# First attention: GpSimd scales the probabilities of 22 units, and scores and turned squares rotate through four and three banks

## The chip, the cores and the metric

The kernel runs on one core of a Trainium2 chip. The metric is device time in microseconds (us), the median of a few executions; lower is better. The engines are named as the profile names them: PE is TensorE (matmuls; PEld its weight loads), DVE is VectorE, ACT is ScalarE, POOL is GpSimd, SP is the engine whose queue starts most of the transfers. PSUM is the memory that PE writes and that DVE and ACT read; the kernel divides it into eight banks.

## The reference

Attention over 4 batches, 8 heads, 768 positions and a head size of 64, in which a position sees itself, the 127 positions before it (the window) and the first 4 positions (the sinks). The result is laid side by side by head (3072 rows of 512) and goes through a gated projection with matrices that arrive as 64-bit floats.

```python
scores = scale * np.matmul(q, k.transpose(0, 1, 3, 2))
keep = is_sink | in_window
scores = np.where(keep, scores, -1000000000.0)
a = np.exp(scores - np.max(scores, axis=-1, keepdims=True))
a = a / (np.sum(a, axis=-1, keepdims=True) + 1e-09)
x = (a @ v).transpose(0, 2, 1, 3).reshape(B * S, H * D)
out = ((x @ w_a) * (x @ w_b)) @ w_out
```

## The kernel before

**Chunks.** The rows are worked in eight chunks of one batch each; the first is batch 0, blocks 0 to 3 of 128 rows (`CHUNKS`). `run` computes the attention of the first chunk by itself (`alone=True`), and from then on the projection of chunk c (`moe`) with the attention of chunk c+1 spread between its matmuls. So the first attention is the only one that has no projection beside it; only the preparation of the first weights and the first products of the projection reach into its end.

**A unit** of the first attention is one head and one block of 128 rows: 8 heads by 4 blocks, 32 units, numbered n = 0 to 31 in the order head by head. Block 0 sees 128 columns (a narrow unit, n divisible by four: 8 of 32); the others see 264 columns: the block before, 8 sink columns and the block itself (24 wide units). `scores` (L601 and on) does for one unit:

- L610, PE: the scores, into a PSUM bank. The banks "s" and "a" take turns, so the scores of unit n+2 wait until those of unit n have been read.
- L617, DVE: adds the mask, takes the extreme of each row, and writes the masked scores `p` to SBUF (one operation and a short one that reads its accumulator).
- L619, ACT: the exponential in place, with the sum of each row beside it.
- L621 and L622, DVE: the sum plus 1e-9, and its reciprocal (one column each).
- L624, DVE: `p` times that reciprocal, in place: the scaling.
- L631, POOL, in blocks 2 and 3 alone (16 of the 32 units): copies the 8 scaled sink columns to `sc`.

`transposes` (L634 and on) turns the scaled `p` on PE (L645; one square for a narrow unit, two for a wide one) into a bank, "t" and "b" in turn, and ACT copies the bank to `pt` (L646). After each second head `av` multiplies the turned squares with the values (L426, 16 matmuls) and ACT copies the product to `xf` (L657); `sinks_t` turns the sink columns (L666, bank "t") and `sinks_av` adds their part (L677 on PE, L679 on DVE). `split_x` then makes two parts of each `xf` for the projection (L720 on ACT, L721 on DVE).

**Order.** `pipeline` issues scores(n), then what is due of `av` and the sinks, then transposes(n-3). That is the order of the code; the framework's scheduler then sets, before the run, the order in which each engine takes its instructions (in the trace L617 of a unit stands ahead of L622 of an earlier one, and L721, which stands behind the whole attention in the code, runs at 21.68 us). At run time each engine takes its own in that order and waits where an input or a buffer isn't ready. Functions marked `keep_in_program_order` keep their order among themselves.

**Banks.** The eight banks are "s", "a", "t", "b", "av", "o0", "o1" and "o2". The projection uses "a" and "b" for its two first products and "o0", "o1", "o2" and "av" for its results; the attention of later chunks uses "s" and "t". During the first attention "o0" to "o2" have held only the warming matmuls at the very start.

**Weights.** From step k = 24 (`STEP0`) of the first attention on, every third step also prepares weights: `weight_bits` (L327 and L329 on DVE, L328 on ACT), `weight_sum` (L336, DVE), `weight_high` (L341, ACT), `weight_low` (L346, DVE). Step k is the one that issues the scores of unit k.

Of the kernel before, what the change touches and what calls it, by code (L numbers as in the profile page):

```python
# [7 lines left out]
F32 = mybir.dt.float32  # L8
# [5 lines left out]
ALU = mybir.AluOpType  # L14
# [5 lines left out]
P = 128  # L20
# [7 lines left out]
SW = 2 * P + NS  # L28
# [5 lines left out]
STEP0, STEPS = 24, 3  # L34
# [182 lines left out]
class Fast:  # L217
# [348 lines left out]
    def parts_exact(self, b, t0, nt, xf, alone, heads, bank):  # L566

        nc = self.nc
        tag = f"{b}_{t0}"
        s0 = max(t0 - 1, 0)  # L570
        nb = t0 + nt - s0
        kw = nb * KB - NS
        late = [i for i in range(nt) if t0 + i >= 2]
        units = [(h, i) for h in heads for i in range(nt)]
        preps, state, sc, vss, skt = {}, {}, {}, {}, {}

        def do_prep(h):
            if h not in heads:
                return
            u = f"{tag}_{h}"  # L580
            if alone:
                pool, at = (self.ld, dict(tag="io", bufs=NIO)) if h % 2 else (self.sp, dict(tag="ks"))
                k = pool.tile([P, MK], F32, name=f"kx{u}", **at)
                q = self.mo.tile([P, nt * P], F32, tag=f"x{'hl'[h % 2]}{h // 2}", name=f"qx{u}", bufs=1)
            else:
                k = self.sp.tile([P, MK], F32, tag="ks", name=f"kx{u}")
                q = self.sp.tile([P, 3 * P], F32, tag=("qh", "ql")[h % 2], name=f"qx{u}")
            nc.sync.dma_start(k[:, :kw], self.kD[b, h, :, s0 * KB:s0 * KB + kw])
            nc.sync.dma_start(q[:, :nt * P], self.qT[b, h, :, t0 * P:(t0 + nt) * P])
            if h % 2 == 0:  # L590
                v = self.sp.tile([P, 2, MB, D], F32, tag="vv", name=f"vx{u}")
                nc.sync.dma_start(v[:, :, :nb], self.vB[b, h // 2, :, :, s0:s0 + nb])
                if late:
                    vs = self.sp.tile([2 * NS, P], F32, tag="vs", name=f"vsx{u}")
                    c = h // 2 % 2
                    nc.sync.dma_start(vs, self.vS[b, h // 4, c * 2 * NS:(c + 1) * 2 * NS, c])
                    vss[h // 2] = vs
            else:
                v = preps[h - 1][2]
            preps[h] = k, q, v  # L600

        def scores(h, i):
            k, q, _ = preps[h]
            t = t0 + i
            u = f"{tag}_{h}_{i}"
            c0 = (max(t - 1, 0) - s0) * KB
            w = SW if t else P
            n = units.index((h, i))
            ps = self.ps.tile([P, SW], F32, tag="sa"[n % 2] if alone else "s", name=f"s{u}")
            nc.tensor.matmul(ps[:, :w], lhsT=q[:, i * P:(i + 1) * P], rhs=k[:, c0:c0 + w], start=True, stop=True)  # L610
            if alone and n % 5 > 2:
                p = self.mo.tile([P, SW], F32, tag=("gh", "gl")[n % 5 - 3], name=f"p{u}")
            else:
                p = self.at.tile([P, SW], F32, tag="p", name=f"p{u}")
            st = self.at.tile([P, 4], F32, tag="st", name=f"st{u}")
            m = (self.m0, self.m1)[t] if t < 2 else self.mg
            nc.vector.tensor_tensor_reduce(out=p[:, :w], in0=ps[:, :w], in1=m, scale=-0.0625, scalar=BIG,  # L617
                                           op0=ALU.add, op1=ALU.min, accum_out=st[:, 0:1])
            nc.scalar.activation(p[:, :w], p[:, :w], AF.Exp, bias=st[:, 0:1], scale=-1.0,  # L619
                                 accum_out=st[:, 1:2])  # L620
            nc.vector.tensor_scalar(st[:, 2:3], st[:, 1:2], 1e-9, None, op0=ALU.add)  # L621
            nc.vector.reciprocal(st[:, 3:4], st[:, 2:3])  # L622
            if alone:
                nc.vector.tensor_scalar(p[:, :w], p[:, :w], st[:, 3:4], None, op0=ALU.mult)  # L624
            else:
                nc.scalar.mul(p[:, :w], p[:, :w], st[:, 3:4])
            state[h, i] = p
            if i in late:
                if h % 2 == 0:
                    sc[h // 2, i] = self.at.tile([P, 2, NS], F32, tag=f"sc{i % 3}", name=f"sc{u}", bufs=2)  # L630
                (nc.gpsimd.tensor_copy if alone else nc.scalar.copy)(sc[h // 2, i][:, h % 2, :], p[:, P:P + NS])  # L631

        def transposes(h, i):
            p = state.pop((h, i))  # L634
            t = t0 + i
            u = f"{tag}_{h}_{i}"
            n = units.index((h, i))
            if alone:
                tp = self.ps.tile([P, 2, P], F32, tag="tb"[n % 2], name=f"t{u}")
            else:  # L640
                tp = self.half_bank(bank, 0, f"t{u}")
            k = max(2 * i - (t0 == 0), 0)
            parts = [p[:, :P]] if t == 0 else [p[:, :P], p[:, P + NS:]]
            for m, part in enumerate(parts):
                nc.tensor.transpose(tp[:, m, :], part, self.ident)  # L645
            nc.scalar.copy(self.turned()[:, h % 2, k:k + len(parts), :], tp[:, :len(parts), :])  # L646

        def av(h):
            if h % 2 == 0:
                return  # L650
            v = preps[h][2]
            if alone:
                ps = self.ps.tile([P, 4, P], F32, tag="av", name=f"av{tag}_{h}")
            else:
                ps = self.half_bank(bank, 1, f"av{tag}_{h}")
            self.values(ps, v, t0, nt)
            nc.scalar.copy(xf[h // 2][:, :nt * P].rearrange("p (c q) -> p c q", q=P), ps[:, :nt, :])  # L657

        def sinks_t(pr):
            n = len(late)  # L660
            if alone:
                tp = self.ps.tile([P, 4, P], F32, tag="t", name=f"skt{tag}_{pr}")
            else:
                tp = self.half_bank(bank, 0, f"skt{tag}_{pr}")
            for k, i in enumerate(late):
                nc.tensor.transpose(tp[:2 * NS, k, :], sc[pr, i].rearrange("p a b -> p (a b)"), self.ident)  # L666
            s = self.at.tile([2 * NS, 3 * P], F32, tag="sct", name=f"sct{tag}_{pr}", bufs=1)
            nc.vector.tensor_copy(s[:, :n * P].rearrange("p (c q) -> p c q", q=P), tp[:2 * NS, :n, :])
            skt[pr] = s

        def sinks_av(pr, _):
            n = len(late)
            if alone:
                ps = self.ps.tile([P, 4, P], F32, tag="av", name=f"sk{tag}_{pr}")
            else:
                ps = self.half_bank(bank, 1, f"sk{tag}_{pr}")
            nc.tensor.matmul(ps[:, :n, :], lhsT=vss[pr], rhs=skt.pop(pr)[:, :n * P], start=True, stop=True)  # L677
            xs = xf[pr][:, late[0] * P:nt * P].rearrange("p (c q) -> p c q", q=P)
            nc.vector.tensor_tensor(xs, ps[:, :n, :], xs, op=ALU.add)  # L679

        return do_prep, scores, transposes, av, sinks_t, sinks_av

    def pipeline(self, units, nt, late, do_prep, scores, transposes, av, sinks_t, sinks_av, lag, group, early):
# [264 lines left out]
```

## Time and profile before

| | us |
|---|---|
| median of 3 executions (771.41 to 772.18) | 771.99 |
| the profiled execution | 771.08 |
| its span in the trace | 769.4 |
| PE busy in the span | 756.9 (98%) |
| DVE, ACT, POOL busy | 396.2, 420.7, 240.8 |

The span is what the trace covers of the profiled execution; 1.7 us of its time lie around it. The page has parts: busy time by engine; the span in slices, with the TensorE clock that was granted; the DMA queues; the chain of work that ended last, followed back from the last instruction; groups of instructions by line with the mean duration of one and the idle time ahead of them. The trace can also be asked for stages (busy time of each engine in a stretch), for waits (who waited for whom) and for the instructions in order of time. A duration there runs from start to end of one instruction; neighbours overlap at their ends, so what one costs its engine is often better read from the distance of two starts. Ends of matmuls are modelled, so a busy PE may still have room.

### The profile page before, as it was taken

The page shows a single profiled execution, that of the slowest core. Times are in us where ns is not written, and L with a number is a line of the kernel's source. Part 1 is how long each engine was busy: PE and PEld are TensorE (multiplying, and loading weights), DVE is VectorE, ACT ScalarE, POOL GpSimd, SP SyncE. Part 2 cuts the span into 40 slices and gives each one's busy share as a digit, 9 for nine tenths or more (in the row PEclk, how much of TensorE's full clock was granted, in tenths as well). Part 3 has the DMA queues.
Part 4 walks back from the last instruction along what each step waited for, and adds up shares of the span by engine and source line. Part 5 has one row for each costly group of instructions (what it writes and reads, how often), then busy time and mean ns, then how long its engine had stood idle before and what let it go on. Part 6 is the DMA issues. An engine that isn't in the chain of part 4 may idle for free.

```text
span 769.4 us, 13051 instructions
## 1 busy us (share of the span) xinstructions
PE 756.9 (98%) x4341; PEld 661.8 (86%) x4341; DVE 396.2 (52%) x1407; ACT 420.7 (55%) x1257; POOL 240.8 (31%) x304
## 2 busy tenths in 40 slices
PE   8999999999999999999999999999999999999997
PEld 4668777789889998999999999999998999899996
DVE  7888999955543443354433454234443445333221
ACT  5875668656645665365434554356663545444431
POOL 1100000244514544165531645224533444102110
PEclk9989999999999999999999999999999999999999
DMA  9996301141221342311211211213333212015511
GB/s 326 340 351 223 128 12 56 55 132 50 60 72 47 120 138 82 125 36 47 59 59 52 60 42 32 63 55 104 111 108 108 67 52 69 1 42 191 167 54 43
DMA packets 44567, 75.78 MB, mean 98 GB/s; under 512 B 4592, under 2 KB 24016, under 8 KB 44496
## 3 DMA queue, kind: packets, MB, share of 16 engines
q1 hardware_dynamic: 41440, 69.40, 27.7%
q10 hardware_dynamic: 3024, 5.51, 1.9%
q8 instruction: 35, 0.57, 0.3%
q14 instruction: 36, 0.29, 0.1%
q0 software_dynamic: 32, 0.00, 0.0%
HBM read 68.60 MB, written 6.29 MB: 97 GB/s over the span
## 4 chain that ended last, share of the span: by engine, by line
PE 96%; DVE 2%; issue 1%; ACT 0%; DMA 0%; POOLq 0%; DVEq 0%; ACTq 0%
PE a L739 26%; PE o L748 26%; PE b L739 26%; PE av L426 5%; PE s L487 5%; PE s L610 2%; PE t L527 1%; PE t L533 1%; PE t L645 1%; DVE p L617 1%; PE t L426 1%; PE skt L548 1%; PE sk L560 0%; DMA nw_raw<-in_nw_dram 0%; DVE p L624 0%
## 5 line engine op out<-in xcount | busy, mean ns | idle before, releaser
L739 PE MATMUL a<-xh,w 128*128 128x384 f32 (+2 forms) x768 | 215.9, 344 | 0.0
L739 PE MATMUL b<-xh,w 128*128 128x384 f32 (+2 forms) x768 | 214.2, 342 | 0.0
L748 PE MATMUL o<-w,gh 128*128 128x512 f32 x576 | 185.3, 403 | 0.0
L739 PEld LDWEIGHTS a<-xh,w 128*128 128x128 f32 x768 | 139.2, 189 | 5.9 <-issue 0.5
L739 PEld LDWEIGHTS b<-xh,w 128*128 128x128 f32 x768 | 139.2, 189 | 3.9 <-issue 0.2
L739 PE MATMUL a<-xl,w 128*128 128x384 f32 (+2 forms) x384 | 129.8, 338 | 0.0
L739 PE MATMUL b<-xl,w 128*128 128x384 f32 (+2 forms) x384 | 129.2, 336 | 0.0
L769 POOL TENSOR_TENSOR gl<-g,gh 128x384 fp32r<-128x384 f32 x60 | 61.0, 1017 | 217.0 <-ACT gh L767 213.3
L764 DVE TENSOR_TENSOR g<-b,g 128x384 f32<-128x384 f32 (+2 forms) x96 | 53.5, 557 | 146.3 <-PE b L739 123.2
L748 PEld LDWEIGHTS o<-w,gh 128*128 128x128 f32 x576 | 103.4, 188 | 19.0 <-issue 0.3
L748 PE MATMUL o<-w,gl 128*128 128x512 f32 x288 | 113.7, 395 | 0.0
L767 ACT CAST gh<-g 128x384 fp32r<-128x384 f32 (+2 forms) x96 | 49.2, 512 | 85.4 <-DVE g L764 83.8
L497 ACT ACTIVATE p<-p,st 128x264 f32<-128x264 f32 (+1 forms) x152 | 65.4, 430 | 50.3 <-DVE st L495 49.6
L758 ACT COPY g<-a 128x384 f32<-128x384 f32 (+2 forms) x96 | 45.3, 472 | 74.7 <-PE a L739 70.1
L739 PEld LDWEIGHTS a<-xl,w 128*128 128x128 f32 x384 | 72.5, 189 | 2.9 <-issue 0.4
L739 PEld LDWEIGHTS b<-xl,w 128*128 128x128 f32 x384 | 72.4, 189 | 2.1 <-issue 0.3
L748 PEld LDWEIGHTS o<-w,gl 128*128 128x128 f32 x288 | 54.1, 188 | 13.6 <-DVE gl L769 0.9
L375 POOL TENSOR_SCALAR ks<-kr 64x400 fp32r<-64x400 f32 (+1 forms) x48 | 28.2, 587 | 106.6 <-DMA kr<-in_kT_dram 103.4
L375 POOL TENSOR_SCALAR qh<-qr 128x384 fp32r<-128x384 f32 x48 | 25.3, 527 | 108.3 <-PE s L487 72.9
L378 POOL TENSOR_TENSOR ks<-kr,ks 64x400 fp32r<-64x400 f32 (+1 forms) x48 | 57.8, 1204 | 3.8
L499 DVE TENSOR_SCALAR st<-st 128x1 f32<-128x1 f32 x152 | 23.2, 153 | 69.0 <-ACT p L497 68.7
L505 ACT ACTIVATE p<-p,st 128x128 f32<-128x128 f32 x96 | 38.7, 403 | 35.1 <-DVE st L500 34.8
(141 smaller groups left out, 1124.2 us busy)
## 6 DMA issues: line engine op xcount, KB each, us to landing
qr<-in_qT_dram SPq DMA_DIRECT2D x48, 192.0 KB, 2.4
raw<-in_wa_dram SPq DMA_DIRECT2D x12, 512.0 KB, 5.9
raw<-in_wb_dram SPq DMA_DIRECT2D x12, 512.0 KB, 6.9
raw<-in_wo_dram SPq DMA_DIRECT2D x12, 512.0 KB, 7.2
chk_a<-in_wa_dram SPq DMA_DIRECT2D x24, 256.0 KB, 3.1
chk_b<-in_wb_dram SPq DMA_DIRECT2D x24, 256.0 KB, 3.1
chk_o<-in_wo_dram SPq DMA_DIRECT2D x24, 256.0 KB, 3.0
out_dram<-os ACTq DMA_DIRECT2D x21, 256.0 KB, 2.2
```

What stands on the lines that cost most here:

```text
L375: self.nc.gpsimd.tensor_scalar(o, i, 1.0, 1.0, op0=ALU.mult, op1=ALU.mult)
L378: (self.nc.vector if self.no_gpsimd else self.nc.gpsimd).tensor_tensor(o, i, high.bitcast(F32), op=ALU.subtract)
L426: self.tc.keep_in_program_order(self.nc.tensor.matmul(ps[e * D:(e + 1) * D, i0:i1, :], lhsT=v[:, e, blk, :], rhs=pt[:, e, sl:sl + i1 - i0, :],
L487: nc.tensor.matmul(ps[:, :w], lhsT=q[:, i * P:(i + 1) * P], rhs=ks[:, c0:c0 + w], start=m == 0, stop=m == 1)
L497: nc.scalar.activation(p[:, :w], p[:, :w], AF.Exp, bias=st[:, 0:1], scale=-1.0, accum_out=st[:, 1:2])
L505: nc.scalar.mul(p[:, NS:KB], p[:, NS:KB], st[:, 3:4])
L739: nc.tensor.matmul(ps[:, :n], lhsT=w[:, ksl], rhs=x[:, :n], start=kk == 0 and i == 0, stop=kk == NK - 1 and i == 2)
L748: nc.tensor.matmul(outs[i], lhsT=g[:, sl], rhs=w, start=j == 0 and k == 0, stop=j == NJ - 1 and k == 2)
L758: nc.scalar.copy(g[:, :n], pa[:, :n])
L764: nc.vector.tensor_tensor(g[:, :n], pb[:, :n], g[:, :n], op=ALU.mult)
L767: nc.scalar.copy(gh[:, :n], g[:, :n])
L769: e.tensor_tensor(gl[:, :n], g[:, :n], gh[:, :n].bitcast(F32), op=ALU.subtract)
```

## The change

The scores of the first attention rotate through four banks ("a", "o0", "o1", "s") where they took turns in two ("s", "a"), and the turned squares through three ("o2", "t", "b") where they took turns in two ("t", "b"). The scaling (L624) of the units n = 0 to 21 is done by POOL; that of the units 22 to 31 stays on DVE. Only the first attention has `alone` set; nothing else changes.

```diff
-            ps = self.ps.tile([P, SW], F32, tag="sa"[n % 2] if alone else "s", name=f"s{u}")
+            ps = self.ps.tile([P, SW], F32, tag=("a", "o0", "o1", "s")[n % 4] if alone else "s", name=f"s{u}")
...
             if alone:
-                nc.vector.tensor_scalar(p[:, :w], p[:, :w], st[:, 3:4], None, op0=ALU.mult)
+                e = nc.gpsimd if n < STEP0 - 2 else nc.vector
+                e.tensor_scalar(p[:, :w], p[:, :w], st[:, 3:4], None, op0=ALU.mult)
             else:
...
             if alone:
-                tp = self.ps.tile([P, 2, P], F32, tag="tb"[n % 2], name=f"t{u}")
+                tp = self.ps.tile([P, 2, P], F32, tag=("o2", "t", "b")[n % 3], name=f"t{u}")
```

## Rows read from the trace of the kernel before

**Rows 1.** the page: the whole span, and each engine's busy time in it

```profile
span 769.4 us, 13051 instructions
...
PE 756.9 (98%) x4341; PEld 661.8 (86%) x4341; DVE 396.2 (52%) x1407; ACT 420.7 (55%) x1257; POOL 240.8 (31%) x304
```

**Rows 2.** stages: PE, PEld, DVE, ACT, POOL busy (instructions); clock, DMA share, GB/s

```profile
7.00:18.00 11.00, 10.33 (x57) 6.41 (x58) 10.40 (x66) 9.05 (x35) 1.15 (x6) 1.00 1.05 394
...
32.00:40.00 8.00, 6.14 (x39) 3.44 (x37) 7.57 (x36) 7.10 (x25) 1.38 (x3) 0.96 1.00 384
...
120.00:128.00 8.00, 8.00 (x47) 6.15 (x45) 7.80 (x16) 6.45 (x15) 0.00 (x0) 1.00 0.01 2
```

**Rows 3.** TensorE's waits from 6 to 150 us: total, times, longest

```profile
PEld s L610 <- DVE st L617: 4.0, 9, 1.5
...
PE s L610 <- DVE st L617: 1.6, 3, 1.1
```

**Rows 4.** the chain that ended last: start us, us, what

```profile
14.43 0.22 PE t L645 x2
...
15.64 0.38 PE skt L666 x2
...
16.02 1.73 PE av L426 x16
...
18.23 0.45 PE s L610 x2
...
18.68 0.62 PE sk L677 x2
...
25.44 1.66 PE av L426 x16
...
33.76 1.66 PE av L426 x16
...
46.64 1.66 PE av L426 x16
```

**Rows 5.** VectorE in order of time: start us, us, engine line operation

```profile
23.07 0.42 DVE L617 CUSTOM_DVE_ANT_0 p<-s,mg 128x264 f32<-128x264 f32 x1
...
23.42 0.35 DVE L624 TENSOR_SCALAR p<-p,st 128x264 f32<-128x264 f32 x1
...
23.69 0.15 DVE L622 RECIPROCAL st<-st 128x1 f32<-128x1 f32 x1
```

**Rows 6.** groups from 6 to 42.5 us: count, busy us, mean ns, idle before

```profile
L624 DVE TENSOR_SCALAR p<-p,st 128x264 f32<-128x264 f32 x22 | 7.6, 350 | 0.1
...
L619 ACT ACTIVATE p<-p,st 128x264 f32<-128x264 f32 x24 | 12.4, 516 | 1.6 <-DVE st L617 1.5
...
L646 ACT COPY pt<-t 128x256 f32<-128x256 f32 x22 | 8.0, 369 | 3.0 <-PE t L645 2.9
```

**Rows 7.** GpSimd's groups over the whole span, same columns

```profile
L375 POOL TENSOR_SCALAR qh<-qr 128x384 fp32r<-128x384 f32 x48 | 25.3, 527 | 108.3 <-PE s L487 72.9 <-issue 33.9 <-DMA qr<-in_qT_dram 0.6
...
L375 POOL TENSOR_SCALAR vs<-vsr 128x256 fp32r<-128x256 f32 x12 | 5.3, 445 | 31.1 <-DMA vsr<-in_vS_dram 16.4 <-issue 8.4 <-PE sk L560 6.3
...
L378 POOL TENSOR_TENSOR ql<-qr,qh 128x384 fp32r<-128x384 f32 x48 | 49.1, 1023 | 2.2
...
L631 POOL COPY sc<-p 128x8 f32<-128x8 f32 x16 | 4.3, 267 | 37.1 <-DVE p L624 16.7 <-DVE st L621 16.5 <-DVE st L622 3.9
```

**Rows 8.** one GpSimd copy, and VectorE's work at that moment (order of time)

```profile
34.91 0.86 POOL L631 COPY sc<-p 128x8 f32<-128x8 f32 x1 [2.58 <-DVE p L624]
...
34.71 0.67 DVE L336 CUSTOM_DVE_ANT_0 wf<-raw,wf 128x1024 uint16<-128x1024 uint16 x1
```

**Rows 9.** the end of the first attention: VectorE, TensorE, and a stage

```profile
40.37 0.35 DVE L624 TENSOR_SCALAR p<-p,st 128x264 f32<-128x264 f32 x1
...
40.86 0.66 PE L645 MATMUL t<-ident,p 128*128 128x128 f32 x2 [1.85 <-DVE p L624]
...
40.00:46.00 6.00, 5.09 (x15) 3.21 (x16) 5.87 (x14) 4.05 (x11) 0.78 (x2) 0.50 1.02 385
```

## Prediction

> **What bounds the kernel now.** I began with the page. PE is busy for 756.9 of 769.4 us [rows 1], so the change can win only where PE is not at its rate, and the first 50 us are the only place where that lasts. The stages show it: in the first attention PE, DVE and ACT all look nearly full (7 to 18 us), near its end DVE is at 7.57 of 8 us and PE at 6.14, and in the first projection PE has 8.00 of 8 with DVE close behind it [rows 2]. A busy PE has modelled ends, though, so I worked out its real need from the chain, where each piece stands at the distance of its successor: two matmuls for the scores of a wide unit 0.45 us, two squares 0.22, and for each second head 1.66 for the values, 0.62 and 0.38 for the sinks [rows 4]. Eight units (two heads, six wide, two narrow at about half) need 6 x 0.45 + 2 x 0.23 + 6 x 0.22 + 2 x 0.11 + 1.66 + 0.62 + 0.38 = 7.4 us. The value products start at 16.02, 25.44, 33.76 and 46.64 us [rows 4]: eight units took 9.4, 8.3 and 12.9 us. So PE was at its rate for only 79% and 89% of the two early stretches.
>
> What else could bound those two? DVE: from start to start a wide unit costs 0.35 for L617, 0.27 for the scaling with the accumulator read [rows 5], and about 0.14 for the two one-column operations (estimated from the 23.69 row's 0.15 with its overlap); a narrow one about 0.5. Eight units are 6 x 0.76 + 2 x 0.5 = 5.6, with some 1.4 for the sinks and L721: 7.0. ACT: 0.516 and 0.369 for a wide unit by their means [rows 6], which count overlaps twice, some 0.6 for a narrow one, 1.1 for the copy of the product and the first part: at most 7.6. All three lie below 9.4 and 8.3. So no engine's total bounds the early stretch; it is the handing over. PE waits 4.0 and 1.6 us (weight loads and matmuls) for L617 to release a score bank [rows 3]: with two banks PE can't put more than two units in front of DVE, and during the 2.7 us of values and sinks DVE and ACT run dry, after which PE waits for them in turn.
>
> The last stretch, 12.9 us, is of another kind: the weights are prepared from step 24 on, DVE is full, a scaling of DVE ends so late that PE waits 1.85 us for it, and for six microseconds after that PE has half its clock, 0.50 of 2.4 GHz [rows 9].
>
> **The change part by part.** *Scaling on POOL.* It takes 22 scalings from DVE, 16 wide and 6 narrow. By the distance of starts that is 16 x 0.27 + 6 x 0.14 = 5.2 us, by the mean of 350 ns at most 22 x 0.35 = 7.7 [rows 5, 6]. It is not path time as such, since DVE's total is not what binds up to 33 us; what it buys is that L617 of the next units no longer stands behind a scaling.
>
> POOL has not done this operation before. Its nearest rows are its two scalings with constants: 445 ns for 256 columns and 527 for 384, from which I take 0.45 for 264 and estimate 0.36 for 128. The bounds are DVE's 0.35 below, since nothing in the trace shows POOL ahead of DVE, and POOL's operation with two full inputs above, 1.02 us for 384 columns [rows 6, 7]. I take 0.45, the row with one input and the nearest width. Eight units are then 6 x 0.45 + 2 x 0.36 and four copies of sink columns at 0.27 [rows 7], 4.5 us of POOL against 7.4 of PE: hidden. At 1.02 it would be 9.2, and POOL itself would bind the stretch; the point between lies near 0.8 us a scaling.
>
> Behind a scaling on POOL stand only the next ones and the sink copies L631, which need the scaled `p` anyway; no transfer is queued there. Who waits is PE, for the transposes. The scaled `p` comes later by 0.45 - 0.35 = 0.1 us a unit, 2.2 us in 22 units if none of it were covered. The cover is the distance of three units between scores and transposes in the code.
>
> *Four score banks.* They add no instruction. The scores of unit n+4 wait for L617 of unit n, not those of n+2. Before values and sinks PE can leave four units with DVE, which with L617 at 0.35 and the small ones at 0.14 is 2.0 us of DVE work against the 2.7 of PE. The waits for L617, 5.6 us by two overlapping views [rows 3], should lose most of their size. What is late next is ACT with its 7.6, or PE itself. More banks only take waits away, so the bound is 0 below, if the planned order of PE doesn't make use of them, and 9.4 - 7.4 and 8.3 - 7.4 above.
>
> *Three banks for the squares.* Transposes wait less for L646. "o0" to "o2" are free until the projection's results, and "a" and "b" are given back by units 28 and 29 where it was unit 31: nothing, and at best the projection's first products start a little earlier. This costs nothing.
>
> *The sum.* I take half of the way to PE's floor: 9.4 to 8.4 and 8.3 to 7.9 are 1.0 and 0.4; the first eight units, whose beginning the masks set, 0.5. The last stretch keeps its DVE work whole, for the units from 22 on and all weights stay there; it starts earlier and I give it 0.6 for the sooner release of banks and for weight work that moves up into DVE's free time. Together 2.5 us. In the projection PE is full, so the gain is kept to the end; the weights are due 2.5 us sooner, and DVE has been relieved of 5.2. The profiled execution takes 771.08 (span 769.4 and 1.7 around it), so 768.6; the median stands 0.9 above the profiled one, so **769.5**.
>
> **The rivals.** *The late stall goes as well.* If the new order brings the last scalings before the weight work, PE's wait of 1.85 us and the half clock behind it can fall: at full clock the 5.09 busy us of that stage would be 2.5 less [rows 9]. DVE is full in that stage (5.87 of 6), which speaks against having all of it, so half of both, 2.2 more: 767.3. With the early stretch at PE's floor it would be about 766.
>
> *Nothing is left of it.* The later arrival of 22 scalings, 2.2 us uncovered, against a gain of 2.5: 771.7. For it speaks that the order of PE is set before the run: if it places a transpose tightly behind a reciprocal, every 0.1 us is felt. The full DVE of the last stretch speaks for it too: what comes early there may only wait for weights. Against it speaks that DVE's own scalings also had to queue behind L617.
>
> *Slower: VectorE's work blocks GpSimd's.* One POOL copy took 0.86 us where the mean is 0.27, and it lies beside L336, a long DVE operation on SBUF [rows 7, 8]: 0.6 us lost. If DVE, now with room, is given its long operations (L721, and the weights L327 to L346) between the units below 22, the scalings are held up by 0.6 each and PE with them. Four on the path take the gain away; eight, as many as one stretch has, cost 4.8 - 2.5 = 2.3 us: 774.3. Against it: before step 24 only L721 is such an operation, and L617 reads the scores from PSUM. The Trainium skill ("SBUF — State Buffer", section "Who interferes with whom") says of this that VectorE and GpSimd share a pair of ports which one instruction holds whole, and that a VectorE instruction with two SBUF inputs keeps GpSimd's reads out, one with a single SBUF input doesn't. By that rule L617 is harmless and L721 and the weight work are not; the copy of 0.86 us agrees, and no run here shows a scaling on POOL yet.
>
> **How the numbers follow.** Forecast, 768 to 770.5: 0.43. Late stall gone, 765.5 to 768: 0.22. Nothing left, 770.5 to 773: 0.19. Slower, 773.5 to 776: 0.16. A measurement of this kernel can tell about 0.2% from no change, 1.5 us. So faster 0.64, same 0.20, slower 0.16. The range takes in the forecast, the third case, most of the second and the low end of the fourth: 766.3 to 773.6, which leaves out some 0.05 below and 0.14 above.
>
> **What would show it.** In the trace after: 22 scalings on POOL at about 0.45 and 0.36 us, ten on DVE; the waits of PE for L617 under 2 us; value products at about 15.5, 23.9, 31.8 and 44 us; PE at 8.00 of 8 from about 47 us. The forecast is wrong if scalings on POOL take over 0.8 us, if PE's waits turn up again as waits of the transposes for POOL, or if the last stretch grows by what the early ones lose. The second case shows as a stage at full clock where 40 to 46 us was at half.

## The result: slower by 0.9%, and the profile after

The changed kernel takes 778.51 us (777.97 to 780.25, 4 executions) against 771.84 of the kernel before beside it: 1.009 times as long, 95% interval 1.0075 to 1.0104. The forecast was 769.5 with a range of 766.3 to 773.6; the loss is 6.7 us. The profiled execution took 778.39, its span is 776.7 (before: 769.4 [rows 1]).

The page of the changed kernel has the same work on PE, and 18 us more on POOL:

```profile
span 776.7 us, 13077 instructions
...
PE 756.0 (97%) x4341; PEld 661.3 (85%) x4341; DVE 391.9 (50%) x1385; ACT 420.8 (54%) x1257; POOL 259.0 (33%) x326
```

22 more instructions for 18.2 us are 0.83 us each, where the sum had 0.45 and 0.36. The groups of the first 50 us name them (count, busy us, mean ns, idle before; L624 and the lines behind it stand one line further down, as L625 and so on); they answer to [rows 6, 7]:

```profile
L625 POOL TENSOR_SCALAR p<-p,st 128x264 f32<-128x264 f32 x16 | 15.0, 945 | 4.2 <-DVE st L621 2.0 <-DVE st L622 1.0 <-ACT pt L647 0.9
L625 POOL TENSOR_SCALAR p<-p,st 128x128 f32<-128x128 f32 x6 | 3.6, 606 | 6.5 <-ACT p L619 5.6 <-DVE st L621 1.0
```

The value products, PE in order of time (start us, us). The kernel before has them at 16.02 and at

```profile
25.37 1.73 PE L426 MATMUL av<-pt,vx 128*64 128x128 f32 x16
33.69 1.73 PE L426 MATMUL av<-pt,vx 128*64 128x128 f32 x16
46.57 1.73 PE L426 MATMUL av<-pt,vx 128*64 128x128 f32 x16
```

(the chain of [rows 4] puts the last three 0.07 later), the changed kernel at

```profile
21.48 1.73 PE L426 MATMUL av<-pt,vx 128*64 128x128 f32 x16
30.22 1.73 PE L426 MATMUL av<-pt,vx 128*64 128x128 f32 x16
38.63 1.73 PE L426 MATMUL av<-pt,vx 128*64 128x128 f32 x16
51.91 2.31 PE L426 MATMUL av<-pt,vx 128*64 128x128 f32 x16
```

Some 5.5 us are lost before the first of them, and they stay lost: 4.9, 4.9 and 5.3 behind the later ones. The distances, 8.7, 8.4 and 13.3, are close to the 9.4, 8.3 and 12.9 of before. So the pipeline has about the old pace once values and sinks take their share of PE; it is slow where it was quick, in the units before the first pair of heads is done. The stages show the engines waiting for each other there (PE 6.44 of 11 us busy where it was 10.33, DVE 5.83 where it was 10.40 [rows 2]) and POOL, hardly used there before, now as busy as any:

```profile
7.00:18.00 11.00, 6.44 (x30) 3.67 (x30) 5.83 (x40) 6.89 (x28) 6.96 (x11) 1.00 0.97 350
...
40.00:48.00 8.00, 3.61 (x19) 1.83 (x15) 7.42 (x29) 5.39 (x18) 0.94 (x2) 0.89 1.04 402
```

(Columns as in [rows 2]: PE, PEld, DVE, ACT, POOL busy; clock, DMA share, GB/s.) Who waited for whom, 0 to 60 us of the changed kernel (us in total, times, longest):

```profile
PEld t L646 <- POOL p L625: 10.0, 15, 1.4
...
DVE p L617 <- POOL p L625: 8.6, 12, 0.9
...
PE t L646 <- POOL p L625: 4.1, 8, 0.7
```

The first and third are the forecast's warning sign: PE's waits for L617 [rows 3] have become waits of the transposes for POOL. The second was not in the forecast at all. L617 reads nothing that POOL writes, yet it waits for POOL twelve times. The order of time shows which scaling it waits for. POOL of the changed kernel (start us, us, instruction, idle before):

```profile
8.93 0.61 POOL L625 TENSOR_SCALAR p<-p,st 128x128 f32<-128x128 f32 x1 [5.57 <-ACT p L619]
10.12 1.87 POOL L625 TENSOR_SCALAR p<-p,st 128x264 f32<-128x264 f32 x2 [0.58 <-DVE st L621]
```

and DVE of the same kernel:

```profile
9.57 0.29 DVE L617 CUSTOM_DVE_ANT_0 p<-s,m 128x128 f32<-128x128 f32 x1 [0.79 <-POOL p L625]
...
11.10 0.43 DVE L617 CUSTOM_DVE_ANT_0 p<-s,m 128x264 f32<-128x264 f32 x1 [0.90 <-POOL p L625]
...
12.02 0.43 DVE L617 CUSTOM_DVE_ANT_0 p<-s,mg 128x264 f32<-128x264 f32 x1 [0.41 <-POOL p L625]
```

The masking of units 4, 5 and 6 starts as the scalings of units 0, 1 and 2 end (9.54, about 11.05, and 10.12 + 1.87 = 11.99). What ties them is `st`, four buffers of four columns: L617 of unit n+4 writes the buffer whose reciprocal the scaling of unit n reads. With both on DVE the order on the engine covered that without a wait; with the scaling on POOL it is a wait across engines, in front of everything that DVE has queued.

The 22 scalings of the changed kernel run from 8.93 to 34.82 us. In the kernel before, those of units 0 to 21 ran on DVE from the first to the second of these rows:

```profile
8.47 0.29 DVE L624 TENSOR_SCALAR p<-p,st 128x128 f32<-128x128 f32 x1
...
28.42 0.35 DVE L624 TENSOR_SCALAR p<-p,st 128x264 f32<-128x264 f32 x1
```

That is 20.3 us before and 25.9 after, and an end 6.0 us later (28.77 and 34.82).

### The profile page after: what moved, and what is told of

It reads as the page before. It is cut to its first block, busy times and chain, and to the rows that moved or that the text cites. A ratio compares the mean times of both kernels' runs of the same rounds, so it can differ in the third digit from the quotient of the medians.

```text
span 776.7 us, 13077 instructions
## 1 busy us (share of the span) xinstructions
PE 756.0 (97%) x4341; PEld 661.3 (85%) x4341; DVE 391.9 (50%) x1385; ACT 420.8 (54%) x1257; POOL 259.0 (33%) x326
## 4 chain that ended last, share of the span: by engine, by line
PE 92%; DMA 2%; POOL 2%; DVE 2%; issue 1%; ACT 1%; SPq 0%; POOLq 0%; DVEq 0%; ACTq 0%
PE o L749 26%; PE a L740 26%; PE b L740 25%; PE s L487 5%; PE av L426 4%; POOL p L625 2%; PE t L527 1%; PE t L533 1%; DMA qx<-in_qT_dram 1%; DMA raw<-in_wa_dram 1%; PE s L610 1%; PE t L646 1%; PE t L426 1%; PE skt L548 1%; PE sk L560 0%
## 5 line engine op out<-in xcount | busy, mean ns | idle before, releaser
L375 POOL TENSOR_SCALAR ks<-kr 64x400 fp32r<-64x400 f32 (+1 forms) x48 | 28.1, 586 | 108.7 <-DVE wf L329 105.6
L375 POOL TENSOR_SCALAR qh<-qr 128x384 fp32r<-128x384 f32 x48 | 25.3, 527 | 108.9 <-PE s L487 73.0
L505 ACT ACTIVATE p<-p,st 128x128 f32<-128x128 f32 x96 | 38.7, 403 | 35.1 <-DVE st L500 34.8
```

Source lines behind the costliest of these rows:

```text
L375: self.nc.gpsimd.tensor_scalar(o, i, 1.0, 1.0, op0=ALU.mult, op1=ALU.mult)
L505: nc.scalar.mul(p[:, NS:KB], p[:, NS:KB], st[:, 3:4])
```

## The experiments

Every time is a median; behind it stand its ratio to the kernel before on the same chip (medians 771.46 to 772.11) and the 95% interval of that ratio. The groups e, f, g and h ran on different chips. The theories: A, the new wait for `st`; B, the price of a scaling; C, the banks; D (from the first four runs on), the early release of banks "a" and "b"; E, an end of the first attention that takes whatever comes early; F, the wait of a scaling for the reciprocal.

**e1_more_st** takes the wait away by more buffers.

```diff
-            st = self.at.tile([P, 4], F32, tag="st", name=f"st{u}")
+            st = self.at.tile([P, 4], F32, tag="sta" if alone else "st", name=f"st{u}", bufs=8 if alone else 4)
```

> The changed kernel, with eight buffers in place of four for the small tile that holds a unit's sum and reciprocal, in the first attention alone. In the changed kernel the masking (L617) of unit n+4 writes the buffer from which GpSimd still reads the reciprocal of unit n, and so waits for that scaling; with eight buffers it does not. Theory A (this new wait is the loss): the 22 scalings took 25.9 us from the first start to the last end, of which GpSimd is busy 20.8 with the sink copies; the 5 us of gaps go, and the time falls from 778.5 to about 773.5. Theory B (the price of a scaling is the loss: 945 ns wide and 606 narrow, where 450 and 360 were forecast): GpSimd stays behind, TensorE waits for it at the transposes as before, and the time stays at 777 to 778.5.

Measured: 776.79 (ratio 1.0065, 1.0049 to 1.0082). L617 no longer waits for POOL's scalings, and 1.7 us come back, not 5. A is real (no execution of the changed kernel is below 777.97, none of e1 above 777.26) and the smaller part.

**e2_banks_only** and **e3_pool_only** do one half of the change each.

> The kernel before with the new banks alone (four for the scores, three for the turned squares); every scaling stays on VectorE. Theory C (the banks, by the other order of TensorE that they bring, are the loss): 776 or more. If the loss is GpSimd's (theories A and B): no slower than 772, and by the forecast's share for the banks, half of the way to TensorE's rate without VectorE's relief, about 770.5.

> The kernel before with the scalings of units 0 to 21 on GpSimd alone; the banks stay at two and two. Theories A and B: as slow as the changed kernel or slower, 778 to 780. Theory C: 772.

Measured: 772.87 (1.0018, 1.0008 to 1.0027) and 775.81 (1.0048, 1.0031 to 1.0065). POOL's scalings are the larger part of the loss, though e3 stays below the 778 to 780 of A and B; and the banks alone don't gain either, against all three theories' figures. Their early gain is there: the value products of e2 on PE start at

```profile
16.21 1.73 PE L426 MATMUL av<-pt,vx 128*64 128x128 f32 x16
24.06 1.74 PE L426 MATMUL av<-pt,vx 128*64 128x128 f32 x16
31.67 1.73 PE L426 MATMUL av<-pt,vx 128*64 128x128 f32 x16
45.01 1.82 PE L426 MATMUL av<-pt,vx 128*64 128x128 f32 x16
```

2.0 us ahead by the third, close to the forecast's 31.8, and 1.6 us ahead at the last. It is spent again in the projection: ACT's copies of its products (L758) are 1.0 us ahead at 65.0 us and 0.3 behind at 75.6. Two things in its trace may stand behind that. PE took a product of the projection with "b" ahead of the last units' transposes, which the early release of "b" made possible, and stood for its weights. The waits of e2 (us in total, times, longest):

```profile
PEld b L739 <- ACT w L341: 1.1, 1, 1.1
...
PE a L739 <- ACT w L341: 1.0, 1, 1.0
```

The second thing is in a stage of e2 far behind the change (columns as in [rows 2]):

```profile
148.00:152.00 4.00, 2.64 (x12) 1.89 (x11) 4.00 (x6) 1.90 (x4) 3.69 (x5) 1.00 0.13 40
```

At 148 to 152 us PE is busy 2.64 of 4 us where the kernel before has 4.00: it waits 1.4 us for L562, an addition for the sinks of the next attention, which DVE starts at 151.15 us behind weight work (149.85 in the kernel before).

**e5_pool_third** is e1 (eight buffers of `st`) with every third unit left to POOL.

```diff
-                e = nc.gpsimd if n < STEP0 - 2 else nc.vector
+                e = nc.gpsimd if n < STEP0 - 2 and n % 3 == 1 else nc.vector
```

> The kernel of the first run, but GpSimd scales only every third unit below 22 (n = 1, 4, 7, ...: seven of them, five wide and two narrow), the rest VectorE. GpSimd then needs 5 x 0.95 + 2 x 0.61 = 6 us for them in some 19, so its price is hidden if nothing else is wrong with it. Theories A and B: the loss is gone, 769 to 771.5. If a scaling on GpSimd hurts by itself, by its later arrival at the transposes, each of the seven costs 0.6 us more than on VectorE: up to 4 us, 774 to 776.

Measured: 770.50 (0.9977, 0.9967 to 0.9987). With seven scalings on POOL the loss is gone and the kernel is a little ahead of the one before. Its trace has the wait of the product with "b" too (1.2 us), and the time is low all the same.

**f1_pool_const** asks what the operation costs by itself. It is e1 without the normalisation of 22 units.

```diff
-                e.tensor_scalar(p[:, :w], p[:, :w], st[:, 3:4], None, op0=ALU.mult)
+                e.tensor_scalar(p[:, :w], p[:, :w], 1.0 if n < STEP0 - 2 else st[:, 3:4], None, op0=ALU.mult)
```

> The kernel of e1_more_st, in which GpSimd multiplies the probabilities of units 0 to 21 by the constant 1 and not by the reciprocal of their sum: it leaves out their normalisation, and a scaling no longer waits for L621 and L622. It puts a price on the operation alone. If the price comes from the factor that is read per row (a column of st), the operation falls from 945 and 606 ns to what the two scalings with constants show, about 450 and 360, and if the price is the whole loss (theory B) the time falls from 776.8 to 770.5 to 772.5. If the price is of GpSimd's in-place work on 264 columns as such, it stays near 945 and 606, and the time at 775 to 777.

Measured: 771.33 (0.9997, 0.9987 to 1.0007), and the price fell by 75 ns alone, to

```profile
L625 POOL TENSOR_SCALAR p<-p 128x264 f32<-128x264 f32 x16 | 13.7, 869 | 0.9 <-ACT p L619 0.9
L625 POOL TENSOR_SCALAR p<-p 128x128 f32<-128x128 f32 x6 | 3.2, 531 | 5.0 <-ACT p L619 4.3 <-PE t L646 0.7
```

That fits neither expectation: the factor read per row is not what makes it dear, and yet 5.5 us went. The run had taken the wait for the reciprocal away as well, so price and wait had to be parted, and the price was still a riddle beside the 527 ns for 384 columns of [rows 7].

**f2_late_banks** tests theory D on the banks alone.

```diff
-tag=("a", "o0", "o1", "s")[n % 4] if alone else "s"
+tag=("o0", "o1", "s", "a")[n % 4] if alone else "s"
...
-tag=("o2", "t", "b")[n % 3]
+tag=("o2", "b", "t")[n % 3]
```

> The kernel of e2_banks_only with the same seven banks in another order: scores rotate through o0, o1, s, a and turned squares through o2, b, t, so that units 31 give back a and b last, as in the kernel before. In e2 the values of the third pair of heads came 2.0 us sooner than before (31.67 against 33.69), and nothing was left of it at 140 us; TensorE had the first product with b queued ahead of the last units' transposes and waited 1.1 and 1.0 us for its weights. Theory D (the early release of a and b put those products into TensorE's queue too soon, and this is what took the early gain away): the products stand behind the last transposes again, and the time falls from 772.9 to 770 to 771. Theory E (the end of the first attention is bound by the weights and VectorE, and whatever comes early waits there): 772 to 773, as e2.

Measured: 770.15 (0.9975, 0.9965 to 0.9986). The product with "b" stands behind the last transposes, the stall at 148 us is gone, and the time is 2.7 us below e2. That is D's figure, but not D's way, for in the trace the early gain isn't kept. The last value products of f2 start at

```profile
46.47 1.74 PE L426 MATMUL av<-pt,vx 128*64 128x128 f32 x16
```

where the kernel before has 46.57 and e2 45.01. The trace is of f2's longest execution (771.67); beyond the 1.4 us of the stall it doesn't show where the 2.7 come from.

**f3_third_old_banks** and **f4_third_late_banks** put seven scalings on POOL together with other banks (and eight buffers of `st`).

> The kernel of e5_pool_third with the banks of the kernel before (two and two). It tells what of the 1.4 us that e5 gained comes from the banks. If GpSimd's seven scalings give the gain by relieving VectorE: 770 to 771. If they only pay together with the banks: 772 to 773, for the waits of the scores for L617 (5.6 us in the kernel before) stay.

> The kernel of e5_pool_third with the banks of f2_late_banks. Theory D: the two gains add up, 768.5 to 769.5. Theory E: no change against e5, 770 to 771.

Measured: 774.90 (1.0029, 1.0016 to 1.0042) and 771.63 (0.9997, 0.9987 to 1.0006). f3 is slower than either expectation. Its trace has the same stall of 1.3 us in the stage from 140 to 160 us as e2, but it is of f3's quickest execution (772.48) and doesn't show what makes the median 774.90. f4 speaks against D: the late banks cost 1.1 us here where they gained 2.7 in f2. So single edits of a microsecond or two in the first 40 us don't add up here; what spends or doubles them later the runs show in part only.

**g1_pool_forms** steps from f1's form to that of the row from which the price was forecast. It too leaves out the normalisation.

```diff
...
+                elif i == 0:
+                    e.tensor_scalar(self.spare[:, :w], p[:, :w], 1.0, None, op0=ALU.mult)
+                elif i == 1:
+                    e.tensor_scalar(p[:, :w], p[:, :w], 1.0, 1.0, op0=ALU.mult, op1=ALU.mult)
+                elif i == 2:
+                    e.tensor_scalar(p[:, :w].bitcast(F32R), p[:, :w], 1.0, 1.0, op0=ALU.mult, op1=ALU.mult)
+                else:
+                    e.tensor_scalar(self.spare[:, :w].bitcast(F32R), p[:, :w], 1.0, 1.0, op0=ALU.mult, op1=ALU.mult)
```

> Only the price of one operation is read from this run. GpSimd multiplies by constants in units 0 to 21 (the normalisation is left out, as in f1_pool_const), in four forms that step from f1's to that of the row from which the price was forecast (two constants, fp32r output, another tile: 0.64 ns a column between 256 and 384): second blocks with two constants in place, float32; third blocks the same with the output written as fp32r; fourth blocks that form into another tile; first blocks (128 columns) with one constant into another tile, float32. f1 showed 869 ns for 264 columns and 531 for 128, one constant in place. If the second constant makes the difference, the second blocks show about 450; if the output type, the third; if work in place, the fourth (and the first about 360). The time of the kernel is not used.

Measured, by its groups on POOL:

```profile
L628 POOL TENSOR_SCALAR spare<-p 128x128 f32<-128x128 f32 x6 | 3.2, 530 | 7.0 <-ACT p L619 6.9
L630 POOL TENSOR_SCALAR p<-p 128x264 f32<-128x264 f32 x6 | 2.5, 414 | 1.1 <-ACT p L619 0.8 <-PE s L610 0.2
L634 POOL TENSOR_SCALAR spare<-p 128x264 fp32r<-128x264 f32 x5 | 2.1, 413 | 0.3
L632 POOL TENSOR_SCALAR p<-p 128x264 fp32r<-128x264 f32 x5 | 2.1, 413 | 1.1 <-ACT p L619 1.1
```

The second operation makes the whole difference. With one operation 128 columns take 530 ns, in place (531 in f1) or not; with two, 264 columns take 414 (869 in f1 with one), whatever the output's type and place. The dear form is the one that does less.

**g3_pool_early** keeps the dear form with a factor per row and takes the wait for the reciprocal away: the factor is another column, and the normalisation is left out.

```diff
-                e.tensor_scalar(p[:, :w], p[:, :w], st[:, 3:4], None, op0=ALU.mult)
+                e.tensor_scalar(p[:, :w], p[:, :w], st[:, 0:1] if n < STEP0 - 2 else st[:, 3:4], None, op0=ALU.mult)
```

> The kernel of e1_more_st, in which GpSimd scales units 0 to 21 by another column of st, the one that L617 wrote (the row's extreme and not the reciprocal of the sum: the normalisation is left out). The price stays that of a factor per row, 945 and 606 ns, but a scaling no longer waits for L621 and L622. e1 (776.8) and f1 (771.3) differ in both. Theory F (the later start of each scaling behind VectorE's two small operations is most of the 5.5 us): 771.5 to 773. Theory B (the price is, even a small part of it, because GpSimd sets the pace): 22 times the 75 ns by which f1 was cheaper are 1.7 us, and the time stays within 2 us of e1, 774.8 to 776.8.

Measured: 773.09 (1.0013, 1.0004 to 1.0023). It lies just above F's range and below B's. Of the 5.5 us between e1 and f1, 3.7 go with the missing wait (its first scaling begins at 7.45 us, that of e1 at 9.95, which is 2.5 of them) and 1.8 with the 75 ns, 22 times. That is how a chain behaves in which POOL has no slack: what moves its start and what moves its price both show in full.

**g5_late_st** and **g8_pool_half** repeat two questions on the kernel of e1.

> The kernel of e1_more_st with the banks in the order of f2_late_banks (a and b given back by unit 31). With every scaling on VectorE that order brought 2.7 us. If the early products of the projection (theory D) add to GpSimd's loss: 774 to 774.5, and the changed kernel's 6.7 us divide into 1.7 for the buffers of st, about 2.5 for the order of the banks and the rest for GpSimd's pace. If GpSimd's late scalings hide it: 776 to 777.

> The kernel of e1_more_st with GpSimd scaling every second unit below 22 (the eleven odd ones, all wide). With its sink copies GpSimd needs 11 x 0.95 + 11 x 0.19 = 12.5 us for them; the scalings of the kernel before took 18.7. If GpSimd hurts only where it sets the pace (a threshold): 770 to 771.5, as with seven units. If every scaling on GpSimd costs by its later arrival, at the rate between none (772.9) and 22 (776.8) of 0.18 us a unit: 774.5 to 775.5.

Measured: 774.66 (1.0035, 1.0021 to 1.0049), 2.1 below e1 and close to D's figure; and 772.75 (1.0007, 0.9997 to 1.0016) with eleven scalings, between the two figures expected and so no verdict on a threshold. It is the time of e2 (772.87), which has none on POOL. (The 18.7 us of that expectation end where unit 20's scaling starts; to the end of unit 21's it is 20.3.)

**h1_two_ops** is the changed kernel with the cheap form, every wait kept. **h2** adds the buffers of e1, **h3** the banks of f2 to that; **h5** is e3 with the cheap form.

```diff
-                e = nc.gpsimd if n < STEP0 - 2 else nc.vector
-                e.tensor_scalar(p[:, :w], p[:, :w], st[:, 3:4], None, op0=ALU.mult)
+                if n < STEP0 - 2:
+                    nc.gpsimd.tensor_scalar(p[:, :w], p[:, :w], st[:, 3:4], 1.0, op0=ALU.mult, op1=ALU.mult)
+                else:
+                    nc.vector.tensor_scalar(p[:, :w], p[:, :w], st[:, 3:4], None, op0=ALU.mult)
```

> The changed kernel with one edit: GpSimd's scaling carries a second operation, times 1.0, so that the instruction has two. In g1_pool_forms two operations took 414 ns for 264 columns and one took 869; with the factor read per row, 75 ns more, the scaling should take about 0.49 us, near the 0.45 of the forecast. If that price is the cause of the loss, the changed kernel's 778.5 fall by most of the 6.7 us, to 770 to 772. If the waits are (L617 behind GpSimd through st, the scaling behind L621 and L622), they stay and the time stays above 775.

> h1 with the eight buffers of st of e1_more_st. With the scaling at 0.49 the wait of L617 of unit n+4 for the scaling of unit n should seldom be last: 0 to 1 us faster than h1, 769.5 to 771.5.

> h2 with the banks in the order of f2_late_banks. Theory D (the early release of a and b costs some 2 to 2.7 us): 768 to 769.5, ahead of both kernels. If the end of the first attention takes whatever comes early: 770 to 771.5.

> The kernel before with GpSimd's scalings of units 0 to 21 in the form with two operations; banks as before, four buffers of st. If the price is the cause of the loss of e3_pool_only (775.8), 771 to 772.5: it should not lose, and gains little, because the scores still wait for their two banks.

Measured: h1 772.87 (1.0014, 1.0004 to 1.0024), h2 772.20 (1.0009, 0.9998 to 1.0021), h3 769.92 (0.9974, 0.9965 to 0.9984), h5 772.37 (1.0005, 0.9995 to 1.0015). The scalings of h1:

```profile
L625 POOL TENSOR_SCALAR p<-p,st 128x264 f32<-128x264 f32 x16 | 7.7, 487 | 4.4 <-DVE st L621 2.9 <-PE s L610 0.7 <-ACT p L619 0.5
L625 POOL TENSOR_SCALAR p<-p,st 128x128 f32<-128x128 f32 x6 | 2.7, 449 | 8.2 <-ACT p L619 6.2 <-DVE st L622 1.5 <-DVE st L621 0.5
```

0.487 is 414 and some 75 for the factor per row. The narrow mean holds one scaling of 0.83 us, which lies beside a long operation of DVE (L721's); in h3 the six take 371. The price alone is 5.6 us of the change's 6.7. The buffers of `st` bring 0.7 more, hardly clear of the spread, and the order of the banks 2.3, and h3 is ahead of both kernels: 0.26% below the one before, 1.1% below the changed one. Its value products stand at

```profile
16.36 1.73 PE L426 MATMUL av<-pt,vx 128*64 128x128 f32 x16
23.31 1.73 PE L426 MATMUL av<-pt,vx 128*64 128x128 f32 x16
31.22 1.73 PE L426 MATMUL av<-pt,vx 128*64 128x128 f32 x16 [0.17 <-ACT pt L649]
```

with 7.0 and 7.9 us between them: on average the pace of PE's 7.4 that the forecast worked out, reached. But e2, with every scaling on DVE, has 7.9 and 7.6, and f2, which is h3 without POOL's scalings, has h3's time: 770.15 and 769.92, ratios 0.9975 and 0.9974. So what h3 gains over the kernel before is the gain of f2's banks. What the scalings on POOL bring by themselves at the cheap price, set against the same banks with all scalings on DVE, is 0.2 us gained with the late banks (f2 and h3), 0.7 gained with the early ones (e2 and h2) and 0.9 lost with the old ones (the kernel before and h5): little that stands clear of the spread. Seven dear ones go from 2.4 gained (e2 and e5) to 3.3 lost (the kernel before and f3).

For the kernels with 22 scalings on POOL, the end of the last one (from the order of time of each) beside the span of the same execution:

| kernel | last scaling ends, us | span, us |
|---|---|---|
| e3_pool_only | 35.7 | 775.4 |
| changed | 34.8 | 776.7 |
| e1_more_st | 32.5 | 774.5 |
| g5_late_st | 32.5 | 772.8 |
| g3_pool_early | 29.8 | 770.8 |
| h5_two_ops_old_banks | 28.8 | 770.7 |
| h1_two_ops | 28.5 | 770.3 |
| f1_pool_const | 28.3 | 769.6 |
| h2_two_ops_st | 26.9 | 770.4 |
| h3_two_ops_st_late | 26.2 | 768.3 |

A microsecond there is about a microsecond at the end. It holds to about 2 us: e3, g5 and h2 lie off it. Each span is of one execution, and executions of one kernel differ by 1 to 2 us.

## Why the prediction was wrong, point by point

**What bounds the early stretches** was right. No engine's total did; two score banks and the handing over did. With four banks alone the products come 2 us sooner by the third pair (e2: 31.67, forecast 31.8). That the two agree is partly luck: the first product of e2 starts at 16.21, not at 15.5, and the stretches behind it take 7.9 and 7.6 us, where half of the way to PE's floor was 8.4 and 7.9.

**The step that failed is the price of a scaling on POOL.** The working had bounds of 0.35 and 1.02 us and took 0.45 "the row with one input and the nearest width" [rows 7]. The rows had the right engine, type of instruction and width, but two operations where the change has one, and that was not looked at. L375 is a helper whose line reads

```python
self.nc.gpsimd.tensor_scalar(o, i, 1.0, 1.0, op0=ALU.mult, op1=ALU.mult)
```

Measured: 0.945 and 0.606. Corrected, the term reads 6 x 0.945 + 2 x 0.606 + 4 x 0.27 = 8.0 us of POOL for eight units, above PE's 7.4: not hidden. All 22 scalings with the ten sink copies between them at 0.19 need 16 x 0.945 + 6 x 0.606 + 10 x 0.19 = 20.7 us, and in the kernel before they took DVE 20.3, from 8.47 to 28.77. So POOL could have kept up only by working without a break, and it had 5.2 us of waits. h1, which changes this term alone, gives 5.6 of the 6.7 us back; the same step with other buffers and banks gives 4.6 (e1 and h2), 4.7 (g5 and h3) and 3.4 (e3 and h5).

**The bound was not carried into the range.** The prediction itself says that POOL would bind above about 0.8 us and that the upper bound would give 9.2 a stretch. That end is a slower kernel; it was given no time and no chance, and the slower rival was built from another mechanism. An estimate from the rows of the kernel before: 22 x 1.02 + 10 x 0.27 = 25.1 us of POOL where DVE took 20.3, an end 4.8 us later, some 777 us. The range ended at 773.6.

**"Behind a scaling on POOL stand only the next ones and the sink copies"** was true of POOL's own queue and missed the other side: who waits for the scaling to be done *reading*. The four buffers of `st` made L617 wait for POOL, 8.6 us in twelve waits, worth 1.7 us (e1) at the dear price and about 0.7 (h2) at the cheap one.

**What the move was to buy** isn't seen either. The prediction said that L617 of the next units would no longer stand behind a scaling, and gave the gain to the whole change. At about the price of the forecast the move gains 0.7 us at most (h2, h3 and h5 against the same banks with all scalings on DVE). What gains in h3 are the banks.

**"More banks only take waits away"** failed too. "a" and "b" are given back by units 28 and 29, and the prediction took that as nothing or a gain. In the run with the banks alone nothing of the 2 us was left at the end, and giving them back last gained 2.7, 2.1 and 2.3 us in three pairs of runs (e2 and f2, e1 and g5, h2 and h3; in ratios to the kernel before 0.43%, 0.30% and 0.35%) and lost 1.1 in one (e5 and f4; 0.20%). That the order of the banks matters is shown. That it acts through the product with "b" that waits for its weights is not shown: e5 has that wait and is quick, and f4 is without it and is slower. The late order also moves "s", "t" and the other banks.

**The rival in which VectorE's work blocks GpSimd's** didn't happen: the median scaling of the changed kernel took 944 ns and the longest 947, so none was held up. The prediction cited a rule of the Trainium skill ("SBUF — State Buffer", section "Who interferes with whom") by which L617, with one input in SBUF, is harmless. The page says it of a VectorE instruction outside the modes that use both ports, an exception that the prediction left out. The trace agrees on L617: it and a scaling of POOL run side by side in the changed kernel at their usual lengths,

```profile
14.27 0.29 DVE L617 CUSTOM_DVE_ANT_0 p<-s,m 128x128 f32<-128x128 f32 x1
```

```profile
14.37 0.94 POOL L625 TENSOR_SCALAR p<-p,st 128x264 f32<-128x264 f32 x1
```

and DVE's waits for POOL go with the buffers of `st` (e1). Where POOL ran beside a long DVE operation with two inputs in SBUF, L721's in g3 at 28.35 us, one scaling took 1.50 us.

**The late stall** didn't go. The changed kernel has it later (columns as in [rows 2]):

```profile
44.00:48.00 4.00, 0.77 (x3) 0.40 (x3) 3.81 (x13) 2.55 (x10) 0.00 (x0) 0.79 1.04 384
48.00:52.00 4.00, 3.61 (x11) 2.06 (x13) 3.00 (x6) 2.64 (x5) 0.78 (x2) 0.50 1.04 400
```

PE stands for most of four microseconds, 2.3 of them for a scaling of DVE, and its granted clock falls to 0.50, as it did from 40 us on before [rows 9]. In f2, h1 and h3 it is 0.50 from 40 to 44 us as well.

**Nothing left of it** was the nearest rival in kind: h1, which is the change at about the price of the forecast, takes 772.87, not 769.5. That is inside the 770.5 to 773 of this rival, and 1.4 us above the kernel before on the same chip.

## What to carry to other kernels

Price an operation that moves to another engine from a row with the same form of instruction, down to the number of operations in it, and if no such row is there, work the upper bound through to a time and give it a chance. Build the change without the move as well: here the banks alone had the whole gain. A dependency that one engine's order covered for nothing becomes a wait once its two ends are on different engines: list every buffer that the moved instruction reads, however small, and who writes it next. And a buffer or bank that comes free sooner can also change the order that the scheduler plans; giving it back last, as in the old order, gained in three pairs of four here.

## What the runs showed of the hardware

A multiplication on GpSimd with one operation in the instruction is slower than the same with a second operation, times one, added: 869 against 414 ns for 264 float32 columns with constants, 945 against 487 with a factor per row. A factor per row instead of a constant adds about 75 ns in either form. The output's type (float32 or fp32r) and whether the work is in place made no difference (413 and 414). With one operation 128 columns take 530 and 264 take 869, 2.5 ns a column. With two operations it is about 0.85: 371 for 128 (h3) and 487 for 264 (h1) with a factor per row. The means of [rows 7], 445 for 256 and 527 for 384, give 0.64, but single long ones (up to 837 ns) are in them; the medians are 407 and 513, 0.83 ns a column.
